# Block linear attention and an ELU feed-forward on one core: attention in visits of two chunks, with half of tile 0's second matmul moved forward

## The chip, the cores and the metric

The kernel runs on one core of one Trainium2 chip. The metric is the device time of one execution in microseconds (us). Each kernel was run several times. The profile of the kernel before shows five engines that work side by side in its span of 246.9 us: TensorE (PE in the profile, busy for 217.1 us, with its weight loads as PEld, 107.1), VectorE (DVE, 163.9), ScalarE (ACT, 137.7), GpSimd (POOL, 51.7) and SyncE (SP, whose queue issues 23 output stores). GpSimd's queue also issues the loads of q, k, v and the weights in this kernel, 50 of them.

## The reference

Cut to what matters: a decaying linear attention for 4 batches and 8 heads, then a two-layer feed-forward with an ELU between.

```python
batch, n_heads, seq, head_dim = (4, 8, 768, 64)       # q, k, v: float32
for b in range(nb):                                    # blocks along the sequence
    intra = einsum('bhic,bhjc->bhij', qb, kb) * Dmask  # decay lam**(i-j), causal
    intra = einsum('bhij,bhjd->bhid', intra, vb)
    inter = einsum('bhid,bhde->bhie', qb * lam_pow, kv_state)
    out[:, :, sl] = intra + inter
    kv_state = lam_block * kv_state + einsum('bhsd,bhse->bhde', kb * rev_pow, vb)
# ... x: [3072 tokens, 512], w_in: [512, 2048], w_out: [2048, 512]
h = x @ w_in
g = where(h > 0, h, exp(minimum(h, 0)) - 1)
return g @ w_out
```

## The kernel before

The sequence is cut into 6 blocks of 128 rows. A "chunk" is one block of one batch, so there are 24 chunks, numbered block by block. Four chunks make one tile of 512 tokens for the feed-forward: six tiles, 0 to 5. The first matmul of a tile has 16 slices of four 128x512 matmuls (`psH`). The second has four blocks of sixteen (`psM`). The attention of tile 0 stands ahead of everything. The attention of tile t+1 stands between the slices of tile t, chunk by chunk: transposes (T), scores (S), the new state (U), the output (O).

```python
def att_T(g):                 # 8 transposes of one chunk into one PSUM bank, tag "A", one buffer
    pt = ps.tile([128, 2, HP, 128], FP16, tag="A", ...)
    ...                       # q^T and k^T copied out by ScalarE (q of tile 0: VectorE)

def att_S(g):
    ...                       # 8 matmuls of 64 rows into two one-bank tiles
    for hh in range(2):       # VectorE: P = S * mask, 512 columns each
        nc.vector.tensor_tensor(out=P[:, hh], in0=ss[hh][:], in1=mask[:, hh], op=ALU.mult)

def att_U(g):
    pu = ps.tile([128, HP, 64], FP32, tag="A", ...)   # the same buffer as T's
    ...                       # 8 matmuls of 64 columns
    for hh in range(2):
        for hp in range(HP):  # VectorE: 8 state updates of 64x64
            nc.vector.scalar_tensor_tensor(out=new[r, hp, r], in0=old[r, hp, r],
                scalar=up[r, h:h+1], in1=pu[r, hp, :], op0=ALU.mult, op1=ALU.add)

def att_O(g): ...             # 8 + 8 matmuls of 64 columns, then one scaling into xt

def mm1(t, n):                # 4 matmuls, then ScalarE: e = exp, r = relu
    ...                       # (in tile 0 every third relu goes to VectorE)
def elu(t, n, e, r):          # VectorE: g = min(e - 1, r), which is the ELU
    nc.vector.scalar_tensor_tensor(out=gt[t][:, n, :], in0=e[:], scalar=-1.0,
                                   in1=r[:], op0=ALU.add, op1=ALU.min)

# tile t's slices; behind each slice four matmuls of the second matmul of tile t-1
```

The kernel's PSUM tiles, counted in banks of 512 float32 columns: one bank for T and U, two for S, one for O, two for `psH` and two for `psM`.

## Time and profile before

Three runs gave 249.97 us (249.71 to 250.82). The profiled span is 246.86 us.

The first thing to read is a table of stretches, cut where each tile's first matmul starts. I took these points from the trace: 23.15, 63.35, 98.18, 133.01, 167.83 and 201.24 us. The columns are the stretch, its length, the busy time of each engine with its number of instructions (PE, PEld, DVE, ACT, POOL), the granted clock of TensorE, the DMA share and GB/s.

```profile
0.00:23.15 23.15, 9.29 (x96) 6.14 (x97) 13.52 (x33) 7.36 (x17) 20.87 (x27) 1.00 1.83 129
23.15:63.35 40.20, 28.27 (x264) 14.38 (x264) 31.20 (x72) 21.95 (x44) 20.56 (x20) 0.92 2.27 176
63.35:98.18 34.83, 34.83 (x288) 17.27 (x288) 28.93 (x67) 22.45 (x44) 10.28 (x9) 1.00 2.42 129
98.18:133.01 34.83, 34.83 (x290) 17.29 (x289) 28.47 (x66) 22.20 (x43) 0.00 (x0) 1.00 0.09 32
```

From tile 1 on TensorE has no gap (34.83 of 34.83 us). Up to there it idles for 14 of 23 us and for 12 of 40 us. The granted clock is part of the picture too: in tile 0 its mean is 0.92. A finer cut of the first half of tile 0 (same columns):

```profile
23.10:43.40 20.30, 13.70 (x108) 6.73 (x107) 11.56 (x24) 10.40 (x22) 10.34 (x11) 0.83 1.57 193
```

Cut finer still, it reads 0.50 from 36.5 to 43 us, just after the longest wait below; the eight first matmuls from 40.34 us on start every 0.40 us there, and every 0.216 us in steady state. As an estimate from the mean, (1 - 0.92) x 40.2 = 3.2 us of full-rate time are missing. What it waits for in tile 0 is shown by the list of TensorE's waits in that stretch (total us, times, longest):

```profile
PE psU L262 <- DVE st L273: 3.7, 1, 3.7
PE psU L262 <- ACT kT L216: 2.9, 2, 1.7
PE psT L207 <- DVE st L273: 2.1, 2, 1.1
```

All three are waits for the one PSUM buffer that U and T share: U waits until the U or T before it has been copied out, T until the U before it has. The longest is not for the buffer alone: VectorE, which had to do the copying out, worked without a pause from 30.50 to 36.59 us. The costliest groups of VectorE, in the listing by form (busy us, mean ns of one | idle before):

```profile
L329 DVE SCALAR_TENSOR_TENSOR g<-e,r 128x512 f16<-128x512 f32 x96 | 65.8, 688 | 47.7 <-ACT r L325 47.2
L247 DVE TENSOR_TENSOR P<-psS,mask 128x512 f16<-128x512 f32 x48 | 30.8, 683 | 2.2 <-PE psS L242 1.9
L273 DVE SCALAR_TENSOR_TENSOR st<-st,up,psU 64x64 f16<-64x64 f16 x128 | 27.8, 279 | 0.2
```

128 state updates take 27.8 us. And one stretch of TensorE in steady state, from the timeline (start, us, line, what, count):

```profile
115.81 0.81 PE L315 MATMUL psH<-xt,wi 128*128 128x512 f16 x3
116.55 0.40 PE L242 MATMUL psS<-qT,kT 64*128 64x128 f16 x8
116.88 0.32 PE L262 MATMUL psU<-vn,kd 128*64 128x64 f16 x8
117.13 1.04 PE L341 MATMUL psM<-wo,g 128*128 128x512 f16 x4
```

### The profile page before, as it was taken

To read this page: it belongs to the slowest core of one execution; us is meant where nothing else is said; L and a number is where in the kernel's file an instruction comes from. 1 tells how busy PE (TensorE), PEld (TensorE's weight loads), DVE (VectorE), ACT (ScalarE), POOL (GpSimd) and SP (SyncE) were. 2 spreads that over 40 slices of the span, in tenths; PEclk is the share of its full clock that TensorE was granted. 3 is DMA by queue.
4 is the path that set the end of the run, shared out by engine and by line. 5 is a ranking of instruction groups with operands and counts; after the bars stand their busy time and mean duration, and the time that the engine had idled before them with its cause. 6 is when DMAs were issued, how large, how long until landed. Compare 5 with 4: busy or idle time off the path is not lost.

```text
span 246.9 us, 4269 instructions
## 1 busy us (share of the span) xinstructions
PE 217.1 (88%) x1664; PEld 107.1 (43%) x1664; DVE 163.9 (66%) x353; ACT 137.7 (56%) x265; POOL 51.7 (21%) x55
## 2 busy tenths in 40 slices
PE   0375748866999999999999999999999999999993
PEld 0243324433445445545544554454454444444441
DVE  6347493999979877977977897787447644444210
ACT  4510735645675576476566656755765757666200
POOL 8996455166551031000000000000000000000000
PEclk9999995999999999999999999999999999999999
DMA  8999999999999979110110111011101101111212
GB/s 51 140 170 171 181 190 206 177 156 147 148 145 170 131 50 123 44 45 0 45 44 9 37 42 43 2 44 45 42 3 42 42 1 45 42 42 42 79 51 85
DMA packets 83924, 20.20 MB, mean 82 GB/s; under 512 B 76096, under 2 KB 80960, under 8 KB 83904
## 3 DMA queue, kind: packets, MB, share of 16 engines
q0 software_dynamic: 80160, 13.63, 87.0%
q1 hardware_dynamic: 3600, 6.17, 6.9%
q8 instruction: 13, 0.21, 0.4%
q10 hardware_dynamic: 144, 0.13, 0.2%
q14 instruction: 7, 0.06, 0.1%
HBM read 27.27 MB, written 6.29 MB: 136 GB/s over the span
## 4 chain that ended last, share of the span: by engine, by line
PE 78%; DVE 12%; DMA 3%; POOL 3%; ACT 2%; issue 1%; POOLq 0%; DVEq 0%
PE psM L341 35%; PE psH L315 31%; PE psT L207 3%; DVE P L247 3%; DMA kn<-in_k_dram 3%; PE psO L286 3%; DVE st L273 3%; DVE g L329 3%; PE psS L242 2%; PE psU L262 2%; DVE xt L299 2%; PE psO L293 2%; POOL qn L73 1%; DVE r L323 1%; DVE kd L223 1%
## 5 line engine op out<-in xcount | busy, mean ns | idle before, releaser
L315 PE MATMUL psH<-xt,wi 128*128 128x512 f16 x384 | 101.2, 388 | 2.5 <-DVE xt L299 1.4
L329 DVE SCALAR_TENSOR_TENSOR g<-e,r 128x512 f16<-128x512 f32 x96 | 65.8, 688 | 47.7 <-ACT r L325 47.2
L320 ACT ACTIVATE e<-psH 128x512 f32<-128x512 f32 x96 | 57.4, 598 | 71.8 <-PE psH L315 65.9
L341 PE MATMUL psM<-wo,g 128*128 128x512 f16 x384 | 96.3, 380 | 0.0
L315 PEld LDWEIGHTS <-wi 128*128 128x128 f16 x384 | 37.4, 100 | 47.9 <-issue 6.8
L325 ACT ACTIVATE r<-psH 128x512 f16<-128x512 f32 x91 | 53.9, 592 | 0.0
L341 PEld LDWEIGHTS <-g 128*128 128x128 f16 x384 | 34.3, 98 | 36.6
L247 DVE TENSOR_TENSOR P<-psS,mask 128x512 f16<-128x512 f32 x48 | 30.8, 683 | 2.2 <-PE psS L242 1.9
L273 DVE SCALAR_TENSOR_TENSOR st<-st,up,psU 64x64 f16<-64x64 f16 x128 | 27.8, 279 | 0.2
L207 PE MATMUL psT<-ident,qn 128*128 128x128 f16 x96 | 10.4, 237 | 10.7 <-DMA qn<-in_q_dram 8.4
L216 ACT COPY kT<-psT 128x512 f16<-128x512 f16 x24 | 14.6, 607 | 9.2 <-DVE qT L212 9.2
L299 DVE TENSOR_TENSOR xt<-psO,qs 128x512 f16<-128x512 f32 x24 | 16.5, 688 | 4.0 <-PE psO L293 2.9
L73 POOL DMA_DIRECT2D qn<-in_q_dram x13 | 14.7, 1131 | 17.5 <-PE psT L207 10.6
L286 PE MATMUL psO<-P,vn 128*64 128x128 f16 x192 | 15.2, 242 | 3.2 <-DVE xt L299 1.7
L73 POOL DMA_DIRECT2D vn<-in_v_dram x13 | 14.6, 1122 | 12.8 <-PE psO L293 7.7
L73 POOL DMA_DIRECT2D kn<-in_k_dram x13 | 14.6, 1123 | 8.0 <-DVE g L329 3.1
L286 PEld LDWEIGHTS <-vn 128*64 128x64 f16 x192 | 10.6, 119 | 11.6 <-issue 11.6
L214 ACT COPY qT<-psT 128x512 f16<-128x512 f16 x20 | 11.8, 591 | 5.7 <-PE psT L207 5.6
L223 DVE TENSOR_TENSOR kd<-kn,ks 128x512 f16<-128x512 f16 x20 | 13.7, 683 | 1.5 <-PE psU L262 1.4
L207 PEld LDWEIGHTS <-qn 128*128 128x128 f16 x96 | 7.6, 104 | 15.9 <-DMA qn<-in_q_dram 8.9
L207 PE MATMUL psT<-ident,kn 128*128 128x128 f16 x96 | 10.4, 238 | 2.7 <-DMA kn<-in_k_dram 2.7
L361 ACT COPY osb<-psM 128x512 f32<-128x512 f32 x12 | 7.1, 591 | 9.6 <-PE psM L341 9.6
(37 smaller groups left out, 90.8 us busy)
## 6 DMA issues: line engine op xcount, KB each, us to landing
out_dram<-osb SPq DMA_DIRECT2D x23, 256.0 KB, 2.0
qn<-in_q_dram POOLq DMA_DIRECT2D x11, 256.0 KB, 12.6
kn<-in_k_dram POOLq DMA_DIRECT2D x11, 256.0 KB, 12.4
vn<-in_v_dram POOLq DMA_DIRECT2D x11, 256.0 KB, 12.5
wo<-in_moe_w_out_dram POOLq DMA_DIRECT2D x4, 512.0 KB, 16.8
wi<-in_moe_w_in_dram POOLq DMA_DIRECT2D x2, 512.0 KB, 12.9
wi<-in_moe_w_in_dram POOLq DMA_DIRECT2D x3, 256.0 KB, 9.5
qn<-in_q_dram POOLq DMA_DIRECT2D x2, 128.0 KB, 4.0
```

Source lines behind the costliest of these rows:

```text
L73: nc.gpsimd.dma_start(out=dst, in_=src[b : b + n, :, rows].rearrange("b h p d -> p (b h) d"))
L207: nc.tensor.transpose(pt[:, j, hp, :], in_=nat[:, 2 * hp : 2 * hp + 2, :], identity=ident16[:])
L223: nc.vector.tensor_tensor(out=dst, in0=heads(kn, g), in1=ks[:].unsqueeze(2).broadcast_to([128, H, 64]), op=ALU.mult,)
L247: nc.vector.tensor_tensor(out=P[:, hh], in0=ss[hh][:], in1=mask[:, hh], op=ALU.mult)
L273: nc.vector.scalar_tensor_tensor(out=new[r, hp, r], in0=old[r, hp, r], scalar=up[r, h : h + 1], in1=pu[r, hp, :], op0=ALU.mult, op1=ALU.add,)
L286: nc.tensor.matmul(po[r, hp, :], lhsT=v_of(g, 2 * hp + hh), rhs=P[:, hh, hp, :], start=True, stop=(c == 0), skip_group_check=True,)
L299: nc.vector.tensor_tensor(out=xt[t][:, :, i * L : (i + 1) * L], in0=po[:], in1=qs[:], op=ALU.mult)
L315: nc.tensor.matmul(pH[:], lhsT=wi[:, kk, j * 128 : (j + 1) * 128], rhs=xt[t][:, kk, :], start=(kk == 0), stop=(kk == HP - 1),)
L320: nc.scalar.activation(e[:], pH[:], AF.Exp)
L325: nc.scalar.activation(r[:], pH[:], AF.Relu)
L329: nc.vector.scalar_tensor_tensor(out=gt[t][:, n, :], in0=e[:], scalar=-1.0, in1=r[:], op0=ALU.add, op1=ALU.min)
L341: nc.tensor.matmul(pm[:], lhsT=gt[t][:, n, i * L : (i + 1) * L], rhs=wo_t[wo_at[n][0]][:, wo_at[n][1], :], start=(n == 0), stop=(n == NF - 1),
```

## The change

Its intent: fewer and larger operations for VectorE and ScalarE, no single PSUM buffer that two steps share, and TensorE's idle time in tile 0 filled with work that was due later. The core of the diff:

```diff
-    NB = 6
+    NB = 12                       # all q/k/v resident
-    LOADS = [..., (2, 2, 'q'), (2, 2, 'k'), (2, 2, 'v'), ('wi', 0), ...]
+    LOADS = [..., (2, 1, 'q'), (2, 1, 'k'), (3, 1, 'q'), (3, 1, 'k'), (2, 1, 'v'), (3, 1, 'v'),
+             ('wi', 0), ..., ('zero',), ('wi', 5), ...]   # weights first; states zeroed by GpSimd
...
+    def visit(g, s0, s1, s2):     # two chunks g, g+1; PSUM tiles of two banks, tag "S", 2 buffers
+        at(s0, att_T, g, 2, "q"); at(s0, att_T, g, 2, "k")
+        at(s0, att_Te, g, 2, "q", "a"); at(s0, att_Te, g, 2, "k", "a")   # 1024 columns each
+        at(s0, att_kd, g, 2)
+        at(s1, att_S, g); at(s1, att_S, g + 1)
+        at(s1, att_mask, g); at(s1, att_mask, g + 1)
+        at(s2, att_tmp, g)        # GpSimd: tmp = old state * decay, for both chunks
+        at(s2, att_O, g, 2); at(s2, att_U, g); at(s2, att_X, g, 2)
+        at(s2, att_st, g)         # VectorE: state = tmp + U, two operations
...
-    if t == 0 and n % 3 == 2: nc.vector.tensor_scalar_max(r[:], pH[:], 0.0)
+    # tile 0, slices 1, 3, 5, 7: no relu; VectorE: m = min(e - 1, 0), g = max(m, h)
...
+    warm(k)                       # nine dummy 128x512 matmuls between tile 0's attention steps
...
+    steps = [..., (('A', 10), (0, 10), [(0, 0, 0), (0, 1, 0)]), ...]
+    # 32 of tile 0's 64 second matmuls, two behind each slice from slice 10 on and in
+    # further steps ("B") without a first matmul; the other 32 two by two in tile 1
```

The tables below call the work up to tile 1's first matmul, with the "B" steps, tile 0's stretch.

## The prediction

> **What bounds the kernel now.** From 63.35 us to the end TensorE is the limit: the table of stretches gives it 34.65 of 34.65 us, 34.90 of 34.90 twice, and the list of waits has no TensorE wait between 70 and 200 us. A 128x512 matmul costs 0.216 us there (four in 0.86 us in the chain of waits). The slack lies before: in 0 to 23.10 us TensorE is busy 9.29 us, in 23.10 to 63.35 us 28.27 of 40.25. From 43.40 to 63.35 us VectorE is busy 19.69 of 19.95 us: it sets the pace of tile 0. The first matmuls start every 0.41 us, twice the later spacing. [...]
>
> **What the change does.**
> 1. Steady state: same TensorE instructions, so no gain in tiles 2 to 5.
> 2. VectorE per two chunks: eight P/xt/kd operations of 512 columns (0.68 us) become four of 1024; from the cost of 512 columns and of 256 (0.42) I estimate 1.2 us each. Sixteen 0.28 us state updates (0.22 apart, 3.5 us per pair) become two of about 0.68. So about 8.8 us become 6.2. The decay product moves to GpSimd.
> 3. Tile 0's exponential/relu: ScalarE gives four relu passes away, VectorE takes about 0.4 us more in each of those slices.
> 4. Startup: q/k of chunks 2 and 3 arrive separately, so chunk 2 no longer waits for the pair; nine dummy matmuls fill TensorE's gaps and should keep the later matmuls at 0.216. First real matmul of tile 0 at about 21.5 us instead of 23.15.
> 5. 32 of tile 0's 64 second matmuls (6.9 us at 0.216) move from tile 1, where TensorE is full, into tile 0's stretch, where it idles.
> 6. Loads: the same bytes, weights first. At the rate of before (170 to 200 GB/s) all first weights land by about 27 us, chunks 4/5 by 33, 6/7 by 40, the second weights by 45; each just in time.
>
> **Sum.** Tile 0 after: the first eleven slices bound by VectorE (about 13 us), to 35; the next five with a visit about 11 us, TensorE and latency; then the stretch without first matmuls about 10 us. Tile 1 starts at about 56 instead of 63.35: 7.4 us. With 6.9 us from tile 1's relief: 14.3 us, all on the critical path. 249.97 - 14.3 = 235.7.
>
> **Prediction:** 235.5 us, 8 in 10 between 230 and 241. Faster by over 2%: 0.93; within 2%: 0.05; slower: 0.02.
>
> **What would show it.** Tile 1's first matmul near 56 us; tile 1's stretch near 28 us instead of 34.65; tiles 2 to 5 unchanged within 1 us; VectorE's total down by about 25 us from 163.9; P and xt near 1.2 us; 0.216 us per matmul from about 22 us on.
>
> **What would make it wrong.** Weights or chunks 4 to 7 late (TensorE waiting for a DMA in tile 0); GpSimd's product stuck behind load issues, holding VectorE's in-order queue in tile 1; [...] the latency of two-chunk visits (transposes, evacuation, scores, mask, output in series) stalling TensorE even in steady state; tile 0's half-rate matmuls returning.

## The result, and the profile after

The changed kernel took 230.85 us (230.47 to 231.08, four runs) against 250.39 us. The ratio is 0.9216, 95% interval 0.9181 to 0.9252. The profiled spans are 246.86 and 228.99 us.

The stretches after, cut in the same way (the columns as above):

```profile
0.00:20.05 20.05, 11.67 (x105) 6.22 (x106) 9.93 (x21) 9.20 (x20) 19.12 (x28) 1.00 1.63 126
20.05:54.00 33.95, 28.74 (x288) 14.86 (x288) 28.63 (x35) 19.60 (x35) 23.13 (x23) 1.00 1.81 173
54.00:83.12 29.12, 27.34 (x257) 14.35 (x256) 22.97 (x28) 20.48 (x36) 23.84 (x22) 1.00 2.43 168
83.12:116.92 33.80, 33.66 (x289) 17.43 (x288) 30.63 (x33) 22.33 (x40) 11.12 (x9) 1.00 0.94 68
116.92:150.40 33.48, 33.48 (x290) 17.32 (x289) 23.94 (x30) 21.78 (x39) 0.00 (x0) 1.00 0.09 33
```

| stretch (us) | before | after | difference | predicted |
|---|---|---|---|---|
| to tile 0's first matmul | 23.15 | 20.05 | -3.10 | -1.65 |
| tile 0 | 40.20 | 33.95 | -6.25 | -5.7 |
| tile 1 | 34.83 | 29.12 | -5.71 | -6.9 |
| tiles 2, 3, 4 | 34.83, 34.82, 33.41 | 33.80, 33.48, 32.97 | -2.81 | 0 |
| tile 5 to the end | 45.62 | 45.62 | 0 | 0 |
| span | 246.86 | 228.99 | -17.87 | -14.3 |

TensorE's waits in tile 0 are smaller now, in none of the longest does T or U wait for the other to be copied out, and the granted clock there is 1.00. The three longest:

```profile
PE psH L351 <- ACT r L360: 1.5, 2, 1.0
PE psU L303 <- DVE kd L223: 1.0, 1, 1.0
PE psH L351 <- DVE g L369: 0.8, 1, 0.8
```

VectorE's groups that answer to those of before:

```profile
L371 DVE SCALAR_TENSOR_TENSOR g<-e,r 128x512 f16<-128x512 f32 x92 | 69.7, 771 | 42.8 <-ACT r L360 42.4
L248 DVE TENSOR_TENSOR P<-psS,mask 128x1024 f16<-128x1024 f32 x20 | 23.5, 1216 | 0.7 <-PE psS L236 0.4
L338 DVE TENSOR_TENSOR st<-tmp,psU 64x512 f16<-64x512 f32 x16 | 10.9, 681 | 4.5 <-POOL tmp L320 4.3
```

The state updates fell from 27.8 to 10.9 us, and 1024 columns cost 1.216 us, as estimated. Two things were not in the prediction's sum. The ELU operation, which nobody touched, became slower: 771 ns instead of 688. And the state updates wait 4.3 us for GpSimd's product (`tmp`). VectorE's total fell by 14.0 us (163.9 to 149.9), not by 25.

Three questions follow. Why did the steady tiles get faster, where the same matmuls run without a gap? What is the earlier start worth? And what holds tile 1 at 29.12 us when TensorE is busy for 27.34?

### The profile page after: what moved, and what is told of

It reads as the page before. It is cut to its first block, busy times and chain, and to the rows that moved or that the text cites. A ratio compares the mean times of both kernels' runs of the same rounds, so it can differ in the third digit from the quotient of the medians.

```text
span 229.0 us, 4114 instructions
## 1 busy us (share of the span) xinstructions
PE 209.5 (91%) x1673; PEld 105.6 (46%) x1673; DVE 149.9 (65%) x191; ACT 135.5 (59%) x243; POOL 77.2 (34%) x78
## 4 chain that ended last, share of the span: by engine, by line
PE 58%; POOL 15%; DMA 12%; DVE 8%; issue 4%; ACT 2%; DVEq 0%; POOLq 0%; ACTq 0%
PE psM L379 29%; PE psH L351 22%; DMA wo<-in_moe_w_out_dram 7%; DMA qn<-in_q_dram 5%; DVE g L371 4%; POOL vn L73 3%; POOL kn L73 3%; POOL qn L73 3%; POOL wi L98 2%; DVE P L248 2%; PE psT L202 2%; POOL tmp L320 2%; POOL st L117 2%; PE psO L261 1%; PE psS L236 1%
## 5 line engine op out<-in xcount | busy, mean ns | idle before, releaser
L351 PE MATMUL psH<-xt,wi 128*128 128x512 f16 x384 | 97.7, 379 | 2.8 <-ACT r L360 1.9
L371 DVE SCALAR_TENSOR_TENSOR g<-e,r 128x512 f16<-128x512 f32 x92 | 69.7, 771 | 42.8 <-ACT r L360 42.4
L248 DVE TENSOR_TENSOR P<-psS,mask 128x1024 f16<-128x1024 f32 (+1 forms) x28 | 28.7, 1064 | 6.3 <-PE psS L236 6.0
L320 POOL TENSOR_TENSOR tmp<-st,up_p 64x512 f32<-64x512 f16 x16 | 20.0, 1250 | 22.7 <-DVE st L338 21.6
L285 DVE TENSOR_TENSOR xt<-psO,qs 128x1024 f16<-128x1024 f32 (+2 forms) x15 | 14.9, 1004 | 6.1 <-PE psO L269 5.4
L213 ACT COPY qT<-psT 128x1024 f16<-128x1024 f16 (+1 forms) x14 | 12.6, 898 | 8.7 <-PE psT L202 8.5
L338 DVE TENSOR_TENSOR st<-tmp,psU 64x512 f16<-64x512 f32 x16 | 10.9, 681 | 4.5 <-POOL tmp L320 4.3
L213 ACT COPY kT<-psT 128x1024 f16<-128x1024 f16 (+1 forms) x14 | 12.8, 917 | 0.0
L223 DVE TENSOR_TENSOR kd<-kn,ks 128x1024 f16<-128x1024 f16 x10 | 12.3, 1230 | 0.0
L397 DVE COPY osb<-psM 128x512 f32<-128x512 f32 x11 | 7.6, 688 | 5.5 <-PE psM L379 5.4
```

Of the source, the lines that this page charges most:

```text
L213: nc.scalar.copy(out=dst[:], in_=pt[:, j])
L248: nc.vector.tensor_tensor(out=P[:, :, c], in0=s[:, :, c], in1=mask[:, :, c], op=ALU.mult)
L285: nc.vector.tensor_tensor(out=xt[t][:, c, i * L : (i + n) * L].rearrange("p h (n l) -> p n h l", n=n), in0=po[:, :, c], in1=qs[:, c].unsqu ...
L320: e.tensor_tensor(out=tmp[r], in0=old[r, :, :, r], in1=up_p[r].unsqueeze(1).unsqueeze(3).broadcast_to([64, 2, HP, 64]), op=ALU.mult,)
L351: nc.tensor.matmul(pH[:], lhsT=wi[:, kk, j * 128 : (j + 1) * 128], rhs=xt[t][:, kk, :], start=(kk == 0), stop=(kk == HP - 1),)
```

## The experiments

All edits are to the changed kernel. Where a run was made once, one trace stands for it. The changed kernel and the "early" kernel below were traced twice each, and their stretches of tile 0 or tile 1 differed by up to 1.6 us between the two traces. Single stretches are read with that in mind. Tile 3 takes 33.47 or 33.48 us in every kernel that keeps the changed kernel's order there. All runs gave a correct result.

### The steady tiles: two chunks' scores in two places

```diff
-        at(s1, att_S, g); at(s1, att_S, g + 1)      # and the masks
+        at(s1, att_S, g); at(s1 + 1, att_S, g + 1)  # from chunk 12 on
-        at(s2, att_O, g, 2)
+        at(s2, att_O, g, 2, part=(0,)); at(s2 + 1, att_O, g, 2, part=(1,))   # U, X, st after it
```

> The changed kernel, but from chunk 12 on the scores of the two chunks stand in two slices and so do the two outputs; the same matmuls, tiles and operations otherwise. Theory A (TensorE loses about 95 ns each time it goes from full-size matmuls to packed ones or back, and the two-chunk visits halve these changes): four more changes in each of six visits, 6 x 0.38 = 2.3 us: tiles 2 and 3 go from 33.80 and 33.48 to about 34.5 and 34.2 us, 233.1 us in all. Theory B (the 1.0 us per tile comes from cheaper evacuation or fewer waits): no wait appears, stretches stay within 0.2 us, 230.9 us.

Measured: 233.96 us, ratio 0.9395 (0.9342 to 0.9447). Tiles 2 and 3 of this kernel:

```profile
83.17:117.52 34.35, 34.35 (x290) 17.07 (x288) 29.86 (x33) 22.55 (x40) 10.22 (x9) 1.00 0.93 67
117.52:151.87 34.35, 34.35 (x289) 17.07 (x288) 24.70 (x31) 21.99 (x39) 1.13 (x1) 1.00 0.09 32
```

Tile 3 went from 33.48 to 34.35 us, with TensorE busy throughout in both. Nothing was added but changes between full-size and packed matmuls; the second chunk's masks also stand a slice later. In the changed kernel one change into scores and one out of them serve 16 score matmuls, not 8 (tile 3, timeline):

```profile
121.70 0.59 PE L351 MATMUL psH<-xt,wi 128*128 128x512 f16 x2
122.23 0.62 PE L236 MATMUL psS<-qT,kT 64*128 64x128 f16 x16
122.78 1.04 PE L379 MATMUL psM<-wo,g 128*128 128x512 f16 x4
```

Distances from one matmul's start to the next, which I computed from the trace in tile 2 of before and tile 3 of after, say what such a change costs. By a change I mean a step between matmuls of different form in the profile: 128\*128 (full-size), 64\*128 (scores) and 128\*64 (state and output), the last two called packed here.

| from, to | before (ns) | after (ns) | without a change (ns) |
|---|---|---|---|
| first matmul to first matmul (128 rows, 512 columns) | 216 | 216 | |
| first matmul to scores (64 rows) | 312 | 312 | 216 |
| scores to state (64 columns) | 146 | none | about 55 |
| scores to second matmul | none | 148 | about 55 |
| first matmul to output (64 columns) | 310 | 309 | 216 |
| output to second matmul | 152 | none | about 53 |
| output to state (both 64 columns) | none | 52 | |
| state to second matmul | 128 | 128 | about 29 |

The last column is the spacing of the same kind of matmul inside its own group; packed matmuls start in pairs 3 to 4 ns apart, and for them it is the usual spacing from one pair to the next. Each change costs about 95 ns (91 to 99 by the table). A chunk of before makes five (to S, S to U, U to second matmul, to O, O to second matmul), so two chunks make ten. A visit of two makes four, because the scores of both stand together and the state follows the output without a change. That is 6 x 95 = 0.57 us for a pair and 1.14 us for a tile with two pairs, of the 1.35 us measured between these two tiles (34.83 to 33.48); the other 0.2 us I did not trace. The experiment adds eight changes to a tile, 0.76 us, and 0.87 was measured. Theory A holds. What TensorE does in these 95 ns is not shown. The profile counts them as busy, because its modelled ends of matmuls cover the gap: in the lines above the first matmuls end at 122.29 us and the scores start at 122.23, though 312 ns lie between the starts.

### The 32 second matmuls, put back

```diff
+    todo = [(0, i, n) for i in range(4) for n in range(NF)]
+    # tile 0's steps: no second matmuls; tile 1's slices: four of todo each
```

> The changed kernel with tile 0's 32 early second matmuls put back into tile 1 (four after each first matmul, as in the later tiles); all else as changed. The prediction counted these 6.9 us in full. Theory A (they fill idle time of tile 0 for nothing): tile 0's stretch stays at 33.9 us, tile 1's grows from 29.1 to 36: about 237.5 us. Theory B (they cost time where they now stand, because the end of tile 0's stretch is a chain of waits with few gaps): tile 0's stretch falls by 2 to 4 us and tile 1's stalls vanish in its longer stretch: 233 to 235 us.

Measured: 236.80 us, ratio 0.9496 (0.9444 to 0.9547). Its tile 0 and tile 1:

```profile
20.24:53.86 33.62, 23.48 (x256) 13.45 (x256) 28.66 (x35) 19.38 (x34) 21.97 (x22) 0.91 1.79 172
53.86:89.39 35.53, 35.53 (x289) 18.41 (x289) 25.46 (x30) 21.56 (x38) 29.65 (x26) 0.94 2.92 163
```

Without them tile 0's stretch is 33.62 us, against 33.95 with them. Tile 1 grew by 6.4 us, and the span by 5.9 (228.99 to 234.92). So the 32 matmuls cost next to nothing where they now stand, as theory A has it; tile 1's gaps did vanish, as theory B has it. Of the 17.87 us they are 5.9. That this is near their 6.9 us of work is partly luck. In this kernel, with TensorE busy for 23.48 us in tile 0 instead of 28.74, the granted clock read 0.50 from 48 to 58 us (its mean over the whole is 0.971 to 0.978 in the four runs, the changed kernel's 0.996 to 1.000). That the smaller load is the cause is not shown. Its tile 1 took 35.53 us where its tile 2 took 33.47, so about 2.1 us went to the low clock, as an estimate (its mean in that tile 1, 0.94, gives (1 - 0.94) x 35.53 = 2.1 as well). The changed kernel's tile 1 lost about as much to waits instead: 29.12 us, against 26.73 in the kernel without these waits (below). The other 11.9 us, this kernel's gain over the kernel before, are 9.5 for tile 1's earlier start (53.86 instead of 63.35 us) and 3.1 in tiles 2 to 4, less 0.7 for a longer tile 1.

### The dummy matmuls

```diff
-    warm(...)        # all six calls, nine matmuls
```

> The changed kernel without its nine dummy matmuls. Theory A (they keep TensorE at its full rate): tile 0's first matmuls start every 0.41 us again as in the kernel before (0.229 us over the first twelve with them), for some 8 to 16 matmuls, and tile 1 starts 1.5 to 3 us later than 54.0; 232 to 234 us against 230.85. Theory B ([...] VectorE's pace hides it): tile 1 starts within 0.5 us of 54.0 or earlier, since up to 0.216 us x 9 of TensorE work is gone; 230 to 231.3 us.

Measured: 230.85 us, ratio 0.9275 (0.9222 to 0.9327). The first is this kernel's start of tile 0 in TensorE's timeline:

```profile
19.25 4.85 PE L351 MATMUL psH<-xt,wi 128*128 128x512 f16 x12 [0.52 <-DVE xt L285]
```

Against the changed kernel:

```profile
20.05 2.75 PE L351 MATMUL psH<-xt,wi 128*128 128x512 f16 x12
```

The half rate did return: twelve matmuls take 4.85 us instead of 2.75. So the dummy matmuls do what they are for. (The granted clock column can't rule such a half rate out: it read 1.00 where the first matmuls of the kernel before came every 0.41 us, from 23.15 us on, and 0.50 from 36.5 to 43 us.) Yet the time is the same. Tile 0's slice 10 is reached at the same 33.44 us in both traces (and at 33.43 or 33.44 in five more whose tile 0 starts between 20.09 and 20.51 us), and tile 1 starts at 53.11 and 54.00 us. Theory A is right about the rate, theory B about the time. The next points say why.

### The loads of chunks 2 and 3 as before

```diff
-    (2, 1, 'q'), (2, 1, 'k'), (3, 1, 'q'), (3, 1, 'k'), (2, 1, 'v'), (3, 1, 'v'),
+    (2, 2, 'q'), (2, 2, 'k'), (2, 2, 'v'),
```

> The changed kernel with chunks 2 and 3 loaded as in the kernel before, in three loads of both. Theory A (the separate loads are what starts tile 0 at 20.05 instead of 23.15 us): tile 0 starts at 22 to 23 us and all that follows shifts by 2 to 3 us: 233 to 234 us. Theory B (it is the new order of TensorE's work, with the outputs behind the scores and the transposes, and the smaller mask pieces): tile 0 starts within 0.8 us of 20.05, 230.5 to 231.7 us.

Measured: 230.07 us, ratio 0.9230 (0.9185 to 0.9275); the changed kernel, in two sets of rounds, 0.9216 and 0.9259. Its tile 0 and tile 1:

```profile
22.43:54.65 32.22, 28.46 (x288) 14.73 (x288) 27.72 (x36) 19.60 (x35) 21.52 (x20) 1.00 1.97 177
54.65:82.10 27.45, 26.83 (x258) 14.26 (x257) 22.75 (x29) 20.52 (x37) 22.63 (x21) 1.00 2.60 168
```

Tile 0 starts at 22.43 us, so the separate loads do start it 2.4 us sooner: theory A's mechanism. But nothing of it arrives. Tile 1 starts 0.65 us later and is 1.7 us shorter, and the whole is not slower. Both theories missed that. In the changed kernel the start is not on the path that ends last: that path runs through GpSimd's load issues, as shown under "The decay products ahead of the loads". Three fewer load issues bring the product of chunk 8 there 1.0 us forward (65.84 instead of 66.86 us), and tile 2 starts 1.0 us sooner (82.10 instead of 83.12).

One place where the early start is lost can be read on VectorE. It is the `m` operation of slice 1, from the timelines of the changed kernel and then of the kernel without dummy matmuls, with the load issue on GpSimd beside it:

```profile
22.52 1.32 POOL L73 DMA_DIRECT2D kn<-in_k_dram  x1
22.84 1.25 DVE L366 TENSOR_SCALAR m<-e 128x512 f16<-128x512 f32 x1
24.13 0.69 DVE L369 TENSOR_TENSOR g<-m,psH 128x512 f16<-128x512 f16 x1
```

```profile
22.52 1.32 POOL L73 DMA_DIRECT2D kn<-in_k_dram  x1
23.49 0.60 DVE L366 TENSOR_SCALAR m<-e 128x512 f16<-128x512 f32 x1 [0.52 <-ACT e L356]
24.13 0.69 DVE L369 TENSOR_TENSOR g<-m,psH 128x512 f16<-128x512 f16 x1
```

The operation takes 0.41 us when it runs free. Here it starts 0.65 us apart in the two kernels and its successor starts at the same 24.13 us, 0.3 us after the load issue ends (spans on GpSimd are rough). The two kernels then run in step up to slice 10. It isn't held every time: in the first trace of the early kernel below it started at 22.70 us beside the same issue and took 0.42; in the second it took 1.22. That the load issue holds the operation, and not something else that ends with it, is inferred from the times; by what means it would do so is not shown.

### Six buffers instead of twelve

```diff
-    NB = 12
+    NB = 6
```

> The changed kernel with six buffers for pairs of chunks as before, instead of all twelve resident. Theory A (no TensorE wait hangs on a load after tile 0, so residency is worth nothing): 230.9 us, within 0.7. Theory B (loads that wait for buffers hold GpSimd's queue, and with it the decay products behind them and VectorE): stalls in tile 1 grow, 232 us or more.

Measured: 231.33 us, ratio 0.9280 (0.9220 to 0.9341), not to be told from the changed kernel. Tile 1's stretch was 30.19 us, within what the changed kernel itself shows (29.12 and 30.69). Keeping everything resident gained nothing that these runs can see, in a kernel whose time up to tile 2 is set elsewhere (next section).

### The decay products ahead of the loads

The chain that ended last in the changed kernel goes back from tile 2 to VectorE and ScalarE in tile 1, and from there to GpSimd's load issues. Further back it goes through loads of chunks and of the second weights, and doesn't touch tile 0's matmuls. Three of its lines (start, us, what), from the chain in order of time:

```profile
21.38 11.19 DMA qn<-in_q_dram
32.85 16.17 DMA wo<-in_moe_w_out_dram
51.17 1.14 POOL kn L73
```

And its lines in tile 1:

```profile
62.22 1.14 POOL kn L73
63.36 1.19 issue
64.55 1.14 POOL vn L73
65.69 0.07 issue
65.75 1.03 POOL tmp L320
66.78 0.07 issue
66.86 1.05 POOL tmp L320
67.93 0.69 DVE st L338
68.65 0.70 DVE g L371
```

In these traces GpSimd does its work in the order of the program: the product for chunk 8, in two halves, starts only when the loads ahead of it have been issued (65.75 us, after an issue that ends at 65.69). VectorE's state update waits for the product (1.90 us), the ELU operations wait behind the state update (an `r` is ready at 66.04 us, its ELU operation starts at 68.65), ScalarE waits for their buffers (2.10 us), and TensorE for ScalarE (0.44 us).

How firmly this held can be checked. Seven traces have these products behind the loads and two second matmuls behind each slice of tile 1: the changed kernel twice, and the runs split scores, no dummy matmuls, loads of pairs, six buffers and, below, all relu passes on ScalarE. Their tile 0 starts between 19.25 and 22.43 us, their tile 1 between 53.11 and 55.87. In all seven, tile 2's first matmul starts 16.26 us after the second half of the product of chunk 8 (at 65.84 to 68.38 us). So GpSimd's queue of loads and products set the time up to tile 2. The runs that "came out the same" were made behind this limit. They show that a part is worth nothing in the changed kernel, not that it would be worth nothing without the limit. The chain also holds 3.63 us of zeroing the states on GpSimd, between weight loads, from 15.75 us on; the change moved this there from VectorE, and no run moved it back.

The edit only moves three products in GpSimd's queue:

```diff
-        at(s2, att_tmp, g)                  # for chunks 6, 8, 10
+    at(("A", 15), att_tmp, 6)               # ahead of the loads of 10 and 11
+    at(("B", 0), att_tmp, 8)                # ahead of the loads of 12 and 13
+    at(("B", 13), att_tmp, 10)              # ahead of the loads of 14 and 15
```

> The changed kernel with the decay products of chunks 6, 8 and 10 issued on GpSimd ahead of the loads that they queued behind; nothing else. Theory A (the queue behind the loads costs tile 1 its 2 us): VectorE's wait for the product in tile 1 falls from 4.3 us to under 1, TensorE's waits there from 2 us to under 1, tile 1's stretch from 29.1 to about 27.5: 229.2 us. Theory B (those waits of VectorE are off the critical path, or the loads come later in exchange): tile 1's stretch within 0.4 us of 29.1, 230.5 to 231.5 us.

Measured: 228.58 us, ratio 0.9157 (0.9098 to 0.9215). Tile 1 of this kernel:

```profile
53.82:80.55 26.73, 26.73 (x257) 14.28 (x256) 23.76 (x30) 20.71 (x37) 19.29 (x17) 1.00 2.37 169
```

TensorE has no gap left in tile 1, and VectorE no longer waits for the product. The difference to the changed kernel is near the noise, so both were run again side by side.

> The changed kernel itself once more, so that it stands on the same chip and in the same rounds as the three beside it. 230 to 231.5 us; tile 0 starts at 20 us, tile 1 at 54, tile 1's stretch 29 to 30.6 us.

> The kernel with the decay products of chunks 6, 8 and 10 ahead of the loads, once more, for a narrow interval beside the changed kernel. If the 26.73 us of tile 1 are real: 228 to 228.8 us, 1% under the changed kernel of these rounds, tile 1's stretch under 27 us.

Measured, five rounds on one chip: the changed kernel 231.08 us, ratio 0.9259 (0.9230 to 0.9287); the early products 229.28 us, ratio 0.9157 (0.9122 to 0.9191). The intervals don't meet. The early products are about 1% faster. Tile 1 was 26.73 us again, against 30.69 us in this trace of the changed kernel. The time missed the 228 to 228.8 us expected; tile 1's stretch did not. Tile 0 of this second trace was 35.14 us instead of 33.91, so part of the gain in tile 1 is given back there; its granted clock read 0.50 from 48 to 51 us, and 1.00 throughout tile 0 in the first trace.

### The decay products on VectorE

```diff
-    def att_tmp(g, eng="p"):
+    def att_tmp(g, eng="v"):
```

> The changed kernel with the decay products on VectorE instead of GpSimd. Theory A ([...] those of tile 1 come late because they queue behind loads): the elu operation's mean falls from 0.771 to 0.69 us, VectorE no longer waits for the product (4.3 us in tile 1), tile 1's stretch falls from 29.1 to 27 to 28 us; 229 to 230 us. Theory B (VectorE's time is what counts, 1.4 us more in each visit): tile 0 and tile 1 grow by 1 to 2 us each; 232 to 234 us.

Measured: 229.73 us, ratio 0.9197 (0.9145 to 0.9248). The ELU operation in this kernel:

```profile
L371 DVE SCALAR_TENSOR_TENSOR g<-e,r 128x512 f16<-128x512 f32 x92 | 62.4, 689 | 46.2 <-ACT r L360 45.9
```

It is back at 689 ns. In the changed kernel's trace, 13 of its 92 ran at the same time as a product on GpSimd: they took 1273 ns on average, and the other 79 took 688. The lines of the changed kernel look like this; four ELU operations take 5.03 us while four products run:

```profile
82.78 5.03 DVE L371 SCALAR_TENSOR_TENSOR g<-e,r 128x512 f16<-128x512 f32 x4
83.25 5.45 POOL L320 TENSOR_TENSOR tmp<-st,up_p 64x512 f32<-64x512 f16 x4
```

Tile 1 fell to 27.53 us, as theory A has it. In time the run is not clearly different from the changed kernel: the interval overlaps both of its ratios' intervals. In the early kernel the ELU operation still averages 761 ns and tile 1 is shorter, so the lateness of the products, not the longer ELU operations, is what cost tile 1 its time.

### All relu passes of tile 0 on ScalarE

```diff
-            er = mm1(t, n, alt=t == 0 and n in (1, 3, 5, 7))
+            er = mm1(t, n, alt=False)
```

> The changed kernel with ScalarE doing all sixteen relu passes of tile 0, so VectorE does one operation in each slice. Theory A (VectorE sets tile 0's pace, ScalarE has room): tile 0's stretch falls by 0.5 to 1.5 us. Theory B (ScalarE sets the pace once its queue has all exponentials and relus, 1.2 us a slice): the first eight slices go from about 1.15 to 1.3 us each, tile 0's stretch grows by 1 to 2 us: 232 to 233 us.

Measured: 231.05 us, ratio 0.9270 (0.9215 to 0.9325). Tile 0's stretch grew to 36.10 us and tile 1's was 28.42, so tile 1 started 1.9 us later (55.87 us). The time can't be told from the changed kernel's. But the traced run is the slowest of the four (232.32 us; the others 230.68 to 231.34), and its granted clock read 0.50 from 32 to 38 us, where it is 1.00 in the changed kernel (the run's mean is 0.984; the others' 0.993 to 1.000). Whether the stretch grew by ScalarE's work, as theory B has it, or by that clock, this trace can't say; the total stays within the noise.

### The state updates as before

```diff
-                nc.vector.tensor_tensor(out=new[r, :, :, r], in0=tmps[g][r], in1=pu[r], op=ALU.add)
+                for i in range(2):
+                    for hp in range(HP):    # old * up + U, 64x64; no product on GpSimd
+                        nc.vector.scalar_tensor_tensor(...)
```

> The changed kernel with the state update as in the kernel before: sixteen small operations on VectorE for a pair of chunks, decay included, none on GpSimd. Theory A (VectorE's operation count sets tile 0's pace, as the prediction had it): 2.1 us more on VectorE in each visit, tile 0's stretch grows by 2 to 4 us; the elu operation falls to 0.69 us and no product is waited for, which gives up to 2 us back in tile 1; tiles 2 to 5 unchanged: 230.5 to 233 us. Theory B (tile 0 is set by other chains): tile 0's stretch grows by under 1 us, and with tile 1's gain the total falls to 228.5 to 230.

Measured: 230.22 us, ratio 0.9213 (0.9185 to 0.9240); the changed kernel beside it 0.9259 (0.9230 to 0.9287). VectorE spends 26.6 us on 128 small updates again, and the kernel is not slower. Tile 0 was 34.65 us, 0.7 to 1.2 more than in the two traces of the changed kernel, and tile 1 28.57. The larger updates take 15.7 us of update work off VectorE (26.6 to 10.9), but its total fell only from 157.7 to 149.9, because 13 of its ELU operations ran longer beside the products (1273 ns against 688, 7.6 us in all), and these products come late in tile 1. On balance they bought nothing in the changed kernel. Theory A's 2 to 4 us in tile 0 did not come, and tile 1 started no later (53.48 us). But the test of VectorE's pace is weak: only one visit's 16 updates and two of the next fall in tile 0's stretch, a wait of 1.3 us for a load of second weights stands in it that the changed kernel's trace doesn't have, and with GpSimd's products gone the chain that ended last does go through these small updates. The early kernel, with large updates and no late product, took 229.28 us in the same rounds, with an interval that just overlaps (0.9122 to 0.9191, against 0.9185 to 0.9240).

### Both: early products and loads of pairs

> The same with chunks 2 and 3 in three loads instead of six. In the changed kernel the three loads of pairs started tile 0 2.4 us later and yet ended 1.4 us sooner. Theory A (fewer load issues only mattered by letting GpSimd's products of tile 1 run sooner): with the products already early the late start shows: tile 1 starts 0.5 to 1.5 us later than in the kernel beside it, 228.8 to 230 us. Theory B (fewer issues bring the weights and chunks of tile 0 sooner, which is worth more): 226.5 to 227.5 us.

Edit: the two edits above together. Measured: 229.25 us, ratio 0.9193 (0.9163 to 0.9223). Tile 1 started at 55.27 us and took 26.73; in the early kernel beside it 55.23 and 26.73. No gain, and no clear loss. Theory B is refused; theory A's late start of tile 1 was not seen in these two traces (the early kernel's first trace started it at 53.82 us). This is the only part taken back with the late products gone.

## Why the prediction was right or wrong

The time, 230.85 us, lies in the range at its lower end. The direction was right, and so was the term for the moved second matmuls. That tile 0's stretch came out near the forecast (33.95 us) confirms no cause, because no run shows what shortened it; as far as is known, this part is luck. The sum was 3.6 us short on the span: 14.3 against 17.87. Point by point:

1. **"Steady state: same TensorE instructions, so no gain in tiles 2 to 5."** Wrong, and the largest miss of the sum: 2.81 us in tiles 2 to 4. The matmuls are the same, but their order has four changes of form for a pair of chunks instead of ten, at about 95 ns each. I took a TensorE without idle time for a floor. The starts in the timeline of before showed it: the scores begin 312 ns after a matmul that needs 216.
2. **VectorE per two chunks, 8.8 to 6.2 us.** The sizes were right (1.216 us for 1024 columns, 0.681 for a state update). That this sets tile 0's pace is not shown: with the small updates back, tile 0 was 0.7 to 1.2 us longer, in a weak test, and the kernel as fast. The total fell by 14.0 us, not 25, partly because 13 ELU operations ran longer beside GpSimd's products: 92 x (0.771 - 0.688) = 7.6 us.
3. **VectorE takes more in four slices of tile 0.** The figure was right where the operation runs free (0.41 us). Two of four took 1.20 and 1.25 us beside load issues. All on ScalarE came out the same in time.
4. **Startup: 21.5 us, on the critical path.** The start came at 20.05, better than predicted. But its worth was misjudged: a start 2.4 us later, and one 0.8 us earlier, both left the time where it was, because the products behind the loads set tile 2's start.
5. **The 6.9 us of moved second matmuls, counted in full.** Nearly right in number, 5.9 us in the span, but two things that the sum left out nearly cancel in it: the low clock without them and the waits of tile 1 with them.
6. **Loads just in time.** No TensorE wait for a load shows in tile 0 after, though the second weights landed at 49.02 us, not by 45. What the loads did cost came by way of GpSimd's queue, in tile 1. Residency had no term in the sum, and six buffers instead of twelve cost nothing that the runs can see.

Tile 1's stretch was predicted near 28 us and was 29.12 and 30.69 in two traces. The reason was among the named risks: "GpSimd's product stuck behind load issues, holding VectorE's in-order queue in tile 1". VectorE's state updates waited 4.3 us for the products there, and ELU operations stood behind them. Moving three products removed it.

What remains open: which part of the new order of attention work brings tile 1's start from 63.35 to 54 us. Taking back the larger state updates, the dummy matmuls, the separate loads, residency or the relu split, one at a time, moved tile 1's start to between 53.11 and 55.87 us. The waits of before point to the single PSUM buffer that T and U shared (3.7 + 2.9 + 2.1 = 8.7 us of TensorE's waits there, absent after). No run gave only the buffer back, so this is argued, not shown. Two rivals stand beside it. VectorE was without a pause in the longest of these waits and busy for 19.69 of 19.95 us from 43.40 us on, so its load may be what counted. And TensorE ran at a granted clock of 0.50 from 36.5 to 43 us, worth up to 3.2 us by the estimate above, where after it is 1.00; the runs of the kernel before whose clock is on record have a mean of 0.955 to 0.986, the changed kernel's 0.996 to 1.000.

## What to carry to other kernels

A TensorE that is busy all the time could still be made faster by its order: here each change of form cost about 95 ns, so group matmuls of one form, and count the changes. Before crediting an earlier start, follow the chain that ended last; here it ran through another engine's queue, and the start was slack. A part that can be taken back at no cost while another limit holds may still count once that limit is gone. Don't put compute that others wait for behind load issues in a queue that is worked in the order of the program, as GpSimd's is in these traces (VectorE waited 4.3 us for its products in tile 1); moving three products forward gained about 1%.
